# Four strided transfers in place of the first load of a one-token decode kernel

## The chip, the core and the metric

The kernel runs on one core of a Trainium2 chip. The engines of the core are TensorE (PE), VectorE (DVE), ScalarE (ACT), GpSimd (POOL) and SyncE (SP); sixteen DMA engines move data between HBM and the on-chip memory SBUF, which has 128 partitions. An instruction on one engine that needs the work of another waits on a semaphore. A transfer adds 16 to its semaphore when all of it has landed. The metric is the device time of one execution in microseconds (us), the median of several.

## What is computed

One token passes through a pre-norm transformer block whose attention reads a long cache of keys and values. All data are float32.

```python
def _A_ref(x, k_cache, v_cache, wq, wo):          # H = 32 heads, Sk = 8192, Dh = 192, D = 640
    q = (x @ wq).reshape(B, Sq, H, Dh).transpose(0, 2, 1, 3)
    scores = jnp.einsum("bhqd,bhkd->bhqk", q, k_cache) * (Dh ** -0.5)
    p = _softmax(scores, axis=-1)
    o = jnp.einsum("bhqk,bhkd->bhqd", p, v_cache)
    return o.transpose(0, 2, 1, 3).reshape(B, Sq, H * Dh) @ wo

h = x + _A_ref(_layernorm(x), A_k_cache, A_v_cache, A_wq, A_wo)
h2 = h + _B_ref(_layernorm(h), B_W_gate, B_W_up, B_W_down)   # gated ReLU, F = 1536
```

Keys and values of 32 heads are 2 x 32 x 8192 x 192 x 4 bytes, about 403 MB; with the weights the kernel reads 446 MB and writes 640 numbers.

## The kernel before

**Layout.** The host packs all inputs into arrays of 128 rows, so that every load takes one contiguous row for each partition. One large buffer, `big`, holds three places for loads (`place[0]` to `place[2]`, line 95), with eight columns ahead of them for x. A head's keys are 12,288 columns, 24 blocks of `QB` = 512 columns that TensorE multiplies with a masked query; its values are 12,288 columns too, which VectorE multiplies with the softmax weights and sums.

**The first array.** `first` holds, for each partition, eight columns with five numbers of x, then `WO` = 960 columns in which the query weights of head 0 lie, then the 12,288 columns of K for head 0, then the query weights of three more heads. It goes to the beginning of `big` in two loads. The first takes `FIRST` columns: x, the query weights and the first four blocks of K (semaphore `w0`). The second takes the rest (semaphore `r1`). Both destinations are the same columns of `big` as the source columns of `first`, so that `FIRST` only sets where the cut lies.

**Order of the loads.** All large loads are issued by SP, one behind the other, in `sync_fn` (the helper `load`, line 156). The start issues `w0`, `r1` and `r2` (values of head 0 and keys of head 1) with no wait between them. After these, `turn` (line 158) issues the loads of three heads for each pass of the loop, eleven passes in all (`NT`); each load waits until the compute engines are done with the place that it overwrites: V's load `r3` waits for `wo`, K's `r4` for `vk`, and so on. The weights of the second half (`ww`) come at the end in six pieces.

**What waits for the first load.** VectorE waits for `w0` (line 263) before it sums x; behind that lie the first layer norm, the five matmuls of head 0's query on TensorE (into `pq`), the columns of the query (`columns`, VectorE) and the masked queries `qs` on ScalarE (`masks`, lines 400 and 401). TensorE then waits for `r1` and for `qs` before the scores of head 0 (`scores`, which go through the helper at line 433). VectorE waits for `r1` before it multiplies the next heads' query weights (`weigh`, line 296). TensorE and VectorE wait for `r1` even for the blocks of K that `w0` has brought.

**Other queues.** ScalarE issues one small load of x for the residual (`xrow`) and one half of the output's store; SP issues the other half (line 188) and waits for both (line 194). GpSimd writes constants at the start and issues no transfer.

Of the kernel before, what the change touches and what calls it, by code (L numbers as in the profile page):

```python
# [10 lines left out]
P, Q, NQ = 128, 32, 4  # L11
# [6 lines left out]
QB = 512  # L18
# [6 lines left out]
WO = D + HN  # L25
# [13 lines left out]
RA, RB = VF + VF, KW + 2 * WO  # L39
R1 = WO + KW + 3 * WQ  # L40
LW = VL + 2 * WO
X0 = 8
FIRST = X0 + WO + 4 * QB

FW = 2 * DJ * F + FJ * D
GATE, DOWN = DJ * F, 2 * DJ * F
# [1 line left out]
CUTS = (0, GATE, DOWN, DOWN + 6 * D, DOWN + 10 * D, FW - HD, FW)  # L48
HOME = (X0 + 2 * RA, X0, X0 + RA + LW)
SCALE = DH ** -0.5  # L50
# [28 lines left out]
def mha_decode_reglu_kernel(nc, x, first, k0, k1, v1, k2, v2, v3, ww, out):  # L79
# [4 lines left out]
    s = {n: nc.alloc_semaphore("e_" + n) for n in names}  # L84
# [3 lines left out]
    def sb(name, shape):  # L88
        return nc.alloc_sbuf_tensor(name, shape, F32).ap()
# [3 lines left out]

    big = sb("big", [P, X0 + 2 * RA + RB])
    place = [big[:, X0:X0 + RA], big[:, X0 + RA:X0 + 2 * RA], big[:, X0 + 2 * RA:]]
    xrow = sb("xrow", [NQ, DG])
# [49 lines left out]
    def home(c0, n):  # L146
        m = min(c0 // GATE, 2)
        return big[:, HOME[m] + c0 - m * GATE:HOME[m] + c0 - m * GATE + n]
# [5 lines left out]
    def sync_fn(sy):  # L154
        def load(n, dst, src):
            sy.dma_start(dst, src).then_inc(s[n], 16)  # L156

        def turn(t, r1):
            sy.wait_ge(s["wo"], t)
            load("r3", place[0], v1[t - 1])  # L160
            sy.wait_ge(s["vk"], 2 * t)
            load("r4", place[1], k2[t - 1])
            load("r5", place[2], v2[t - 1])
            sy.wait_ge(s["op"], 3 * t)
            load("r1", place[0][:, 0:r1], k0[t - 1][:, 0:r1])
            sy.wait_ge(s["sp"], 3 * t)
            load("r2", place[1], k1[t])

        load("w0", big[:, 0:FIRST], first[:, 0:FIRST])
        load("r1", big[:, FIRST:X0 + R1], first[:, FIRST:])  # L170
        load("r2", place[1], k1[0])
        with sy.Fori(1, NT - 1) as t:
            turn(t, R1)
        turn(NT - 1, WO + KW + WQ)
        sy.wait_ge(s["wo"], NT)
        load("r3", place[0][:, 0:VF], v1[NT - 1][:, 0:VF])
        load("r3b", place[0][:, VF:], v1[NT - 1][:, VF:])
        sy.wait_ge(s["vk"], 2 * NT)
        load("r4", place[1][:, 0:LW], v3)
        for i, (c0, c1) in enumerate(zip(CUTS, CUTS[1:])):  # L180
            if c0 == GATE:
                sy.wait_ge(s["op"], H)
            load(f"ffn{i}", home(c0, c1 - c0), ww[:, c0:c1])
# [64 lines left out]
    def vector_fn(v):  # L248
# [11 lines left out]
        v.sem_inc(s["op"], 1)  # L260

        s1, mean, s2, var, rstd = (st[:, i:i + 1] for i in range(4, 9))
        v.wait_ge(s["w0"], 16)
        v.reduce_sum(s1, xT, axis=AX.X).then_inc(s["st"])
        v.wait_ge(s["st"], 2)
        stat(v.tensor_scalar_mul(mean, pt[:, 0:1], 1.0 / D))
# [252 lines left out]
    def tensor_end(t):  # L519
# [27 lines left out]
        ins.then_inc(s["pd"])  # L547

    sync_fn(nc.sync)
    scalar_fn(nc.scalar)  # L550
    pool_fn(nc.gpsimd)
    vector_fn(nc.vector)
    tensor_fn(nc.tensor)
    tensor_end(nc.tensor)
# [6 lines left out]
def _pack(x, k, v, wq, wo, up, gate, down):  # L561
# [23 lines left out]
    rows = [_np.zeros(z, k.dtype) for z in ((NT - 1, P, R1), (NT, P, RA), (NT, P, RA), (NT - 1, P, RA), (NT - 1, P, RB))]  # L585
    first = _np.zeros((P, X0 + R1), k.dtype)
    first[:, 0:DJ] = x.reshape(P, DJ)
# [43 lines left out]
```

## Time and profile before

| quantity | value |
|---|---|
| median of three runs | 1037.24 us (1037.07 to 1037.32) |
| device time of the profiled execution | 1037.36 us |
| its span in the profile | 1036.0 us |
| mean granted TensorE clock | 0.641 of full speed |
| read from HBM | 445.91 MB, 430 GB/s over the span |
| large loads: K, V, weights of the second half | 31, 23 and 6, beside the two of `first` |

A row of the page's groups gives the line, the engine, the operation and what it writes and reads. In the windows, each row gives a stretch's start and end, its length, the busy time of PE, weight load, DVE, ACT and POOL (with the count of instructions), the granted TensorE clock, the mean busy share of the DMA engines and the GB/s that they moved. In short windows the DMA columns scatter, since a packet's bytes are booked over its recorded time and some records overlap. In the timeline, the first two columns are start and duration; in brackets stands how long the engine had been idle and what released it. The list of DMA issues gives the size and the median time from issue to landing. The chain of waits is followed back from the last instruction, and its rows are start, length and what it was spent on.

### The profile page before, as it was taken

The page shows a single profiled execution, that of the slowest core. Times are in us where ns is not written, and L with a number is a line of the kernel's source. Part 1 is how long each engine was busy: PE and PEld are TensorE (multiplying, and loading weights), DVE is VectorE, ACT ScalarE, POOL GpSimd, SP SyncE. Part 2 cuts the span into 40 slices and gives each one's busy share as a digit, 9 for nine tenths or more (in the row PEclk, how much of TensorE's full clock was granted, in tenths as well). Part 3 has the DMA queues.
Part 4 walks back from the last instruction along what each step waited for, and adds up shares of the span by engine and source line. Part 5 has one row for each costly group of instructions (what it writes and reads, how often), then busy time and mean ns, then how long its engine had stood idle before and what let it go on. Part 6 is the DMA issues. An engine that isn't in the chain of part 4 may idle for free.

```text
span 1036.0 us, 6215 instructions
## 1 busy us (share of the span) xinstructions
PE 337.1 (33%) x2104; PEld 104.0 (10%) x2104; DVE 604.5 (58%) x1288; ACT 61.0 (6%) x145; POOL 3.5 (0%) x18
## 2 busy tenths in 40 slices
PE   3413323143323134240523322233315133231527
PEld 2100100010001001010100000010101001010103
DVE  3555737645675656476555747645666557376582
ACT  1000000000000000000000000000000000000010
POOL 1000000000000000000000000000000000000000
PEclk9756665666657566655666575666657566656667
DMA  9999999999999999999999999999999999999998
GB/s 400 444 443 418 430 443 424 456 410 443 440 441 410 438 445 441 410 449 431 443 410 439 441 443 430 417 444 443 411 437 443 443 415 432 443 424 439 428 433 348
DMA packets 8948, 445.98 MB, mean 430 GB/s; under 512 B 1000, under 2 KB 1136, under 8 KB 1264
## 3 DMA queue, kind: packets, MB, share of 16 engines
q1 hardware_dynamic: 8932, 445.92, 99.6%
q8 instruction: 3, 0.05, 0.0%
q14 instruction: 1, 0.01, 0.0%
q10 hardware_dynamic: 12, 0.00, 0.0%
HBM read 445.91 MB, written 0.00 MB: 430 GB/s over the span
## 4 chain that ended last, share of the span: by engine, by line
DMA 81%; DVE 10%; PE 8%; issue 0%; SPq 0%; ACT 0%
DMA big<-in_k_dram 76%; DVE big L151 9%; PE sp L433 8%; DMA big<-in_ww_dram 3%; DMA big<-in_v_dram 2%; PE pq L433 0%; DVE mp L315 0%; SPq L156 0%; DVE op L151 0%; PE acc L433 0%; PE pt L473 0%; ACT o L429 0%
## 5 line engine op out<-in xcount | busy, mean ns | idle before, releaser
L151 DVE CUSTOM_DVE_ANT_0 big<-big,p 128x1024 f32<-128x1024 f32 x384 | 445.0, 1221 | 276.3 <-DMA big<-in_v_dram 173.1
L433 PE MATMUL sp<-big,qs 128*32 128x512 f32 x1536 | 266.1, 858 | 398.7 <-DMA big<-in_k_dram 253.3
L433 PEld LDWEIGHTS sp<-big,qs 128*32 128x32 f32 x1536 | 60.0, 147 | 573.8 <-issue 256.8
L433 PE MATMUL po<-op,same 128*128 128x13 f32 x66 | 17.6, 343 | 237.8 <-DVE op L151 237.8
L405 ACT ACTIVATE p<-sp,m 128x1024 f32<-128x1024 f32 x32 | 35.7, 1114 | 928.7 <-DVE m L319 928.7
L315 DVE TENSOR_REDUCE mp<-sp 128x1 f32<-128x1024 f32 x32 | 39.2, 1225 | 55.9 <-PE sp L433 55.9
L433 PEld LDWEIGHTS po<-op,same 128*128 128x128 f32 x66 | 14.6, 274 | 251.2 <-DVE op L151 242.8
L288 DVE SCALAR_TENSOR_TENSOR big<-big,xn 128x576 f32<-128x576 f32 x44 | 35.8, 813 | 0.4
L296 DVE TENSOR_SCALAR big<-big,xn 128x576 f32<-128x576 f32 x11 | 6.8, 618 | 44.0 <-DMA big<-in_k_dram 37.2
L151 DVE DVE_READ_ACCUMULATOR2_ANT op<- 128x1 f32 x384 | 31.8, 83 | 0.0
L473 PE MATMUL pt<-ident,mp 128*128 128x128 f32 x32 | 11.1, 346 | 40.2 <-DVE mp L315 40.2
L291 DVE SCALAR_TENSOR_TENSOR big<-big,o 128x640 f32<-128x640 f32 x22 | 19.3, 878 | 0.0
L151 DVE CUSTOM_DVE_ANT_0 junk<-ident,pq 128x128 f32<-128x128 f32 x34 | 9.7, 285 | 11.1 <-PE pq L433 11.1
L243 DVE RECIPROCAL rl<-po 128x1 f32<-128x1 f32 x33 | 5.4, 165 | 13.0 <-PE po L433 13.0
L151 DVE CUSTOM_DVE_ANT_0 junk<-blk,po,rl 128x8 f32<-128x8 f32 x66 | 11.9, 218 | 1.2
L433 PE MATMUL pq<-big,ones 128*128 128x384 f32 (+1 forms) x44 | 12.5, 406 | 0.0
L292 DVE SCALAR_TENSOR_TENSOR big<-big,o 128x320 f32<-128x320 f32 x22 | 12.0, 545 | 0.0
L319 DVE TENSOR_REDUCE m<-pt 128x1 f32<-128x128 f32 x32 | 9.3, 290 | 4.6 <-PE pt L473 4.6
L400 ACT ACTIVATE qs<-pick,q 128x64 f32<-128x64 f32 x34 | 11.5, 338 | 3.8 <-DVE q L151 3.8
L473 PEld LDWEIGHTS pt<-ident,mp 128*128 128x128 f32 x32 | 4.5, 140 | 68.6 <-DVE mp L315 68.6
L401 ACT ACTIVATE qs<-pick,q 128x32 f32<-128x32 f32 x34 | 10.4, 306 | 0.0
L433 PE MATMUL sp<-big,hc 128*32 128x384 f32 x80 | 9.3, 616 | 0.6 <-DVE hc L371 0.6
(88 smaller groups left out, 106.7 us busy)
## 6 DMA issues: line engine op xcount, KB each, us to landing
big<-in_k_dram SPq DMA_DIRECT2D x9, 8064.0 KB, 31.0
big<-in_v_dram SPq DMA_DIRECT2D x10, 7104.0 KB, 45.7
big<-in_v_dram SPq DMA_DIRECT2D x2, 4096.0 KB, 22.7
big<-in_ww_dram SPq DMA_DIRECT2D x2, 3840.0 KB, 27.1
big<-in_k_dram SPq DMA_DIRECT2D x1, 7104.0 KB, 28.9
big<-in_first_dram SPq DMA_DIRECT2D x1, 6560.0 KB, 20.9
big<-in_v_dram SPq DMA_DIRECT2D x1, 3008.0 KB, 17.3
big<-in_ww_dram SPq DMA_DIRECT2D x1, 1920.0 KB, 32.4
```

The costliest lines, as they stand in the source:

```text
L151: return eng.tensor_tensor_reduce(out=res, in0=a, in1=b, scale=scale, scalar=0.0, op0=ALU.mult, op1=ALU.add, accum_out=dst)
L288: return v.scalar_tensor_tensor(tq, wqs[:, :, j, :], xn[:, j:j + 1], tq, op0=ALU.mult, op1=ALU.add)
L291: v.scalar_tensor_tensor(tw[:, 0:D], wos[i][:, 0:D], o[:, i, 0:1], tw[:, 0:D], op0=ALU.mult, op1=ALU.add)
L292: return v.scalar_tensor_tensor(tw[:, D:WO], wos[i][:, D:WO], o[:, i, 1:2], tw[:, D:WO], op0=ALU.mult, op1=ALU.add)
L296: v.tensor_scalar_mul(tq, tq, xn[:, 0:1]).then_inc(s["pr"])
L315: v.reduce_max(mp, sp, axis=AX.X).then_inc(s["mp"])
L319: v.reduce_max(m1, pt[:, 0:P], axis=AX.X, negate=True).then_inc(s["m1"])
L400: a.mul(qs[:, i, 0:2, :], pk[:, 0:2, :], q[:, i, 0:1])
L401: a.mul(qs[:, i, 2, :], pk[:, 2, :], q[:, i, 1:2]).then_inc(s["qs"])
L405: a.activation(p, sp, AF.Exp, bias=m1, accum_out=op[:, i, NJ:NJ + 1]).then_inc(s["rs"])
L433: return nc.tensor.matmul(dst, lhsT, rhs, start=start, stop=stop, **kw)
L473: t.transpose(pt[:, 0:P], mp.to_broadcast([P, P]), ident).then_inc(s["pt"])
```

## The change

`FIRST` grows from four to eight blocks of K, so that the cut between the two loads of `first` moves from column 3016 to column 5064. The load of the part ahead of the cut becomes four loads on the same queue and the same semaphore. Each takes a set of partitions at a regular step: partitions 0, 8, 16, ... (16 of them), then 4, 12, 20, ... (16), then 2, 6, 10, ... (32), then 1, 3, 5, ... (64). Together they are all 128. VectorE's wait for `w0` asks for 64 instead of 16. The loads behind them, their order and their waits stay.

```diff
 R1 = WO + KW + 3 * WQ
 LW = VL + 2 * WO
+LANES = ((0, 8), (4, 8), (2, 4), (1, 2))
 X0 = 8
-FIRST = X0 + WO + 4 * QB
+FIRST = X0 + WO + 8 * QB
...
-        load("w0", big[:, 0:FIRST], first[:, 0:FIRST])
+        for p0, step in LANES:
+            load("w0", big[p0:P:step, 0:FIRST], first[p0:P:step, 0:FIRST])
         load("r1", big[:, FIRST:X0 + R1], first[:, FIRST:])
         load("r2", place[1], k1[0])
...
-        v.wait_ge(s["w0"], 16)
+        v.wait_ge(s["w0"], 16 * len(LANES))
```

## The prediction

> **What bounds the kernel now.** I read the page first (engines' shares, queues), then the windows at the start and in the middle, the list of DMA issues, the start of the chain of waits and the timeline of the first 35 us, and last the end of the chain.
>
> ```profile
> span 1036.0 us, 6215 instructions
> PE 337.1 (33%) x2104; PEld 104.0 (10%) x2104; DVE 604.5 (58%) x1288; ACT 61.0 (6%) x145; POOL 3.5 (0%) x18
> ...
> q1 hardware_dynamic: 8932, 445.92, 99.6%
> ...
> DMA 81%; DVE 10%; PE 8%; issue 0%; SPq 0%; ACT 0%
> ```
> ```profile
> 0.00:2.00 2.00, 0.00 (x0) 0.00 (x0) 0.00 (x0) 0.58 (x1) 1.40 (x10) 1.00 0.20 37
> 2.00:4.00 2.00, 0.00 (x0) 0.00 (x0) 0.00 (x0) 0.70 (x1) 1.86 (x9) 1.00 0.85 308
> ...
> 100.00:900.00 800.00, 249.33 (x1487) 71.64 (x1487) 476.82 (x996) 42.51 (x104) 0.00 (x0) 0.63 1.00 433
> ```
>
> The queue that SP feeds is busy for 99.6% of the span on sixteen engines; no compute engine is above 58%. In the 800 us from 100 to 900 the DMA share is 1.00 at 433 GB/s, which is 433 / 16 = 27.1 GB/s for each DMA engine. So the chain's DVE and PE pieces lie beside a stream that never stops, and the kernel is as long as the stream: 445.92 MB at 433 GB/s are 1029.8 us. What remains of 1036.0 lies at the two ends. For that I need when the transfers were issued and landed.
>
> ```profile
> big<-in_first_dram SPq DMA_DIRECT2D x1, 6560.0 KB, 20.9
> ...
> big<-in_first_dram SPq DMA_DIRECT2D x1, 1508.0 KB, 5.9
> ```
> ```profile
> 0.81 0.42 SPq L156
> 1.23 0.06 issue
> 1.29 0.41 SPq L156
> 1.70 0.05 issue
> 1.75 40.50 DMA big<-in_k_dram
> ...
> 1032.35 0.04 issue
> 1032.39 1.93 PE pq L433 x56
> 1034.34 0.30 ACT o L429
> ```
>
> The first transfer (1508 KB) is issued at 0.81 and lands 5.9 us later, at 6.71. The second (6560 KB) is issued at 1.29 and lands at 22.19. Between the two landings 6.72 MB arrive in 15.48 us, 434 GB/s: the stream is at its steady rate right behind the first transfer. At that rate the first one's 1.544 MB take 3.56 us, so 5.9 - 3.56 = 2.34 us of its time is start: issue, first bytes, ramp and notice of landing. The tail, from the last large landing on the chain (1032.35) to 1036.0, is 3.65 us. Together 0.81 + 2.34 + 1029.8 + 3.65 = 1036.6, 0.6 over the span because the last weights still arrive within the tail. Whatever the change does to the start of the stream therefore moves the end by as much.
>
> **The change, part by part.** My sums are made against the profiled execution: span 1036.0, device time 1037.36 (1.36 beside the span). The median is 1037.24, 0.12 lower; I add the difference to the median.
>
> *Bytes.* The four transfers carry 20,256 B a partition, 2532 KB; the second falls from 6560 to 5536 KB. The sum is 8068 KB before and after: 0.
>
> *Issues.* SP issues three more. From the chain rows, one costs 0.42 + 0.06 us, so the second transfer goes out at 1.29 + 3 x 0.47 = 2.70 and K's next block at 3.16 instead of 1.75. The cover is the data of the four: 5.97 us at 434 GB/s. A 16-row transfer has, if it is spread over all sixteen engines, one row of 20,256 B for each, 0.75 us at 27.1 GB/s; that is longer than the 0.47 to the next issue, so no engine runs dry between them: 0. Without that cover the three would cost 1.41.
>
> *Completions.* Three more sets of sixteen. The 433 GB/s of the long window already contains those of its transfers; its rounding (0.5 in 433, 1.2 us over the kernel's 62 loads) leaves at most 0.02 each, or 0.06 us; I take that.
>
> *The later x.* VectorE's wait is now for 64 increments, all four transfers. Behind it in VectorE's queue are the layer norm and the first query, and TensorE and ScalarE wait for those. x comes 1024 KB later, 2.42 us.
>
> ```profile
> 6.75 0.16 DVE L264 TENSOR_REDUCE st<-big 128x1 f32<-128x5 f32 x1 [0.84 <-DMA big<-in_first_dram]
> ...
> 15.19 0.31 ACT L401 ACTIVATE qs<-pick,q 128x32 f32<-128x32 f32 x1
> ...
> 22.23 0.62 DVE L296 TENSOR_SCALAR big<-big,xn 128x576 f32<-128x576 f32 x1 [6.84 <-DMA big<-in_first_dram]
> ...
> 22.25 7.40 PE L433 MATMUL sp<-big,qs 128*32 128x512 f32 x48 [7.59 <-DMA big<-in_first_dram]
> ...
> 33.22 0.34 SPq L156 DMA_DIRECT2D big<-in_v_dram  x1
> ```
>
> The chain from x to the masked query ends at 15.50, and both engines then wait for the second transfer until 22.23. The slack is 6.7 us; 2.42 fit into it: 0. If the four transfers are slow, the second one lands late by the same amount, so the slack never falls under 6.7 - 2.4 = 4.3. Nor does the stream run dry later: V's first load is issued at 33.22 while K's block lands at 1.75 + 40.50 = 42.25, 9.0 us ahead, and both shift together.
>
> *The ramp* is what can be won. A small transfer that has almost no data shows the part of the 2.34 us that a transfer pays at any rate:
>
> ```profile
> 1034.67 0.34 SPq L188 DMA_DIRECT2D out_dram<-o  x1
> ```
> ```profile
> SPq L194 <- DMA out_dram<-o: 0.9, 1, 0.9
> ```
>
> The 1.2 KB store takes 0.34 + 0.9 = 1.24 us from issue to landing. So the ramp is at most 2.34 - 1.24 = 1.10 us, and a gain has that as its end; the other end is 0. The window from 2 to 4 us runs at 308 instead of 433: 125 x 2 us = 250 KB, 0.58 us. With one row an engine in the first transfer the engines may start closer together, but a first row must still be fetched from cold. I take -0.4, most of the 0.58 and not the 1.10.
>
> *The rate of part transfers* is the cost that decides, and the trace of before has no row for it: every load that fills the stream has 128 rows, and 433 GB/s is known for those alone. From below: the engines run at 27.1 GB/s whichever partitions they write, cost 0. From above: a transfer with every eighth partition reaches only half of SBUF's receiving side. If the 433 GB/s are sixteen receiving shares of 27.1, of which sixteen engines in a whole transfer take one each, then two engines meet at one share, the other shares stand idle, and the rate is 217. The engines work their queue in order, so the first two transfers (16 rows, 0.324 MB each) cost 0.75 more each, 1.49 together. In the 32-row and the 64-row transfer each engine has two and four rows. If an engine's rows follow each other in the transfer, all engines write first one half of the shares and then the other, and these double too: 1.49 and 2.99 more. All four: 5.97 us. An upper end that needs no such picture is a whole start for each added transfer, 3 x 2.34 = 7.0 (rival c); the two agree in size. Engines that are out of step relieve this: one that is 0.2 us ahead leaves the shared half 0.2 us earlier, at each of the six stretches (one, one, two, and two double ones), 1.2 us in all; the 0.2 is an estimate, a third of the ramp's 0.58. I take 5.97 - 1.2 = 4.8, near the upper end: a rate of exactly sixteen equal parts looks like a fixed share for each engine, and nothing in the diff keeps two engines off one share.
>
> [...]
>
> **The sum:** 0 + 0 + 0.06 + 0 - 0.4 + 4.8 = +4.5 us. Span 1040.5; on the median 1037.24 + 4.5 = **1041.7 us**.
>
> **The rivals.** About 0.2% (2.07 us) is what a measurement of this kernel can tell from no change; it lies at 1035.17 and 1039.31.
>
> (a) *Ramp alone, not slower.* Place: the first 4 us. Each engine gets its first row early, and any 16 engines run at 27.1 GB/s. For it speaks the window at 308 GB/s; against it that the stream then needs a rate which the trace shows for 128 rows only. Price -0.4 (0 to -1.1): 1036.8 (1036.1 to 1037.2). It decides if the part transfers keep over 95% of 433 GB/s (5% of 5.97 us is 0.3). That the split does nothing at all, since the engines take rows in the same way as before, ends here too.
>
> (b) *Only the two 16-row transfers are at half rate*, since with 32 and 64 rows the engines already spread over all shares at any moment: +1.49 + 0.06 - 0.4 = +1.1: 1038.4. [...] Against: it needs an order of rows in the engines that suits the stride.
>
> (c) *Each transfer pays a start of its own*, not hidden under the one ahead: 3 x 1.24 - 0.4 = +3.3: 1040.6. Against it: the second transfer follows the first at 434 GB/s, so its start was hidden under 3.6 us of data; the 16-row ones have only 0.75 us ahead of them. At most 3 x 2.34 = +7.0.
>
> (d) *Over 2.07 us won.* Needs more than the whole ramp of 1.10; only a change of the tail could add to it.
>
> **How the numbers follow.** Forecast 0.46, (a) 0.20, (b) 0.24, (c) 0.06, (d) 0.04. The forecast's own range runs from six tenths of the doubling (5.97 x 0.6 - 0.4 = +3.2, 1040.4) to all of it without relief and no ramp gain (+6.0, 1043.2). The whole range reaches down into (a), to 1036.5, leaving out (d) and the better half of (a), and up to 1043.0. Slower: the forecast less 0.02 for its mild end, and (c): 0.50. Within 0.2%: (a), (b) and that rest: 0.46. Faster: (d), 0.04.
>
> **What would show it.** Issue rows: four of `first` at 0.81, 1.28, 1.75, 2.2 and the 5536 KB one at about 2.7. The last of the four should land near 0.81 + 2.34 - 0.4 + 5.97 + 4.8 = 13.5 us (VectorE's first reduce on x at L264's place); by (a) at 8.7, by (b) at 10.2, by (c) at 12.1. The 5536 KB transfer, then, lands 5.669 MB / 434 = 13.1 us after it, 26.6 instead of 22.2, and every later landing is late by the same 4.5. The windows from 4 to 12 us should show some 220 to 260 GB/s. Wrong would be: windows back at 433 by 4 us; a first reduce before 9 us; a later landing that moves by another amount than the second transfer's; or VectorE and TensorE waiting for the masked query instead of for the second transfer at L296 and L433.

## The result, and the profile after

The changed kernel takes 1038.88 us (median of 22 runs, 1038.46 to 1039.63), the kernel before 1037.22 in the same sessions (22 runs, 1036.97 to 1037.48). The ratio is 1.0016, 95% interval 1.001 to 1.0023: 1.66 us slower, within 0.2%. The forecast was +4.5, so its direction holds and its size doesn't; rival (b) with +1.1 comes nearest.

The page of the changed kernel (span; busy time by engine; the load queue's packets, MB and share; the chain by engine):

```profile
span 1037.6 us, 6218 instructions
PE 334.1 (32%) x2104; PEld 103.5 (10%) x2104; DVE 604.3 (58%) x1288; ACT 61.0 (6%) x145; POOL 3.5 (0%) x18
...
q1 hardware_dynamic: 8980, 445.92, 99.5%
...
DMA 81%; DVE 10%; PE 8%; SPq 0%; issue 0%; ACT 0%
```

Nothing has changed in what bounds it: the same 445.92 MB, in 48 packets more (three completions on sixteen engines), the same 58% of VectorE. The windows of the start and of the middle, read as before (the last column is GB/s):

```profile
2.00:4.00 2.00, 0.00 (x0) 0.00 (x0) 0.00 (x0) 0.69 (x1) 1.86 (x9) 1.00 1.24 304
4.00:6.00 2.00, 0.00 (x0) 0.00 (x0) 1.53 (x8) 0.00 (x0) 0.26 (x1) 1.00 0.72 192
...
6.00:9.00 3.00, 0.00 (x0) 0.00 (x0) 0.00 (x0) 0.00 (x0) 0.00 (x0) 1.00 1.00 425
...
100.00:900.00 800.00, 247.16 (x1487) 71.32 (x1487) 478.12 (x998) 42.50 (x104) 0.00 (x0) 0.63 1.00 434
```

The steady stream runs at 434 GB/s, as it did at 433. The stretch from 4 to 6 us, in which the second 16-row transfer and the first rows behind it are moved, shows 192; from 6 to 9, where the 32-row and the 64-row transfer are under way, it is 425 already. The loss is made in about the first 6 us and then stays. (Such short windows scatter; the lengths of single packets, further down, say the same without that.) The list of DMA issues and the timeline say the same by landings:

```profile
big<-in_first_dram SPq DMA_DIRECT2D x1, 5536.0 KB, 20.5
...
big<-in_first_dram SPq DMA_DIRECT2D x1, 1266.0 KB, 8.1
big<-in_first_dram SPq DMA_DIRECT2D x2, 316.5 KB, 4.6
big<-in_first_dram SPq DMA_DIRECT2D x1, 633.0 KB, 5.7
```
```profile
10.82 0.16 DVE L266 TENSOR_REDUCE st<-big 128x1 f32<-128x5 f32 x1 [4.91 <-DMA big<-in_first_dram]
...
19.25 0.31 ACT L403 ACTIVATE qs<-pick,q 128x32 f32<-128x32 f32 x1
...
23.91 0.62 DVE L298 TENSOR_SCALAR big<-big,xn 128x576 f32<-128x576 f32 x1 [4.46 <-DMA big<-in_first_dram]
...
23.93 1.94 PE L435 MATMUL sp<-big,qs 128*32 128x512 f32 x8 [5.21 <-DMA big<-in_first_dram]
...
34.74 0.35 SPq L157 DMA_DIRECT2D big<-in_v_dram  x1
```

VectorE's first use of the second transfer (L298 here, L296 before) moves from 22.23 to 23.91, by 1.68. V's first load goes out at 34.74 instead of 33.22, by 1.52, and the span ends 1.6 later. One delay at the start is passed through the whole kernel. The masked query ends at 19.56, and both engines wait for the second transfer for 4.4 us more, so that the later x costs nothing.

### The profile page after: what moved, and what is told of

It reads as the page before. It is cut to its first block, busy times and chain, and to the rows that moved or that the text cites. A ratio compares the mean times of both kernels' runs of the same rounds, so it can differ in the third digit from the quotient of the medians.

```text
span 1037.6 us, 6218 instructions
## 1 busy us (share of the span) xinstructions
PE 334.1 (32%) x2104; PEld 103.5 (10%) x2104; DVE 604.3 (58%) x1288; ACT 61.0 (6%) x145; POOL 3.5 (0%) x18
## 3 DMA queue, kind: packets, MB, share of 16 engines
q1 hardware_dynamic: 8980, 445.92, 99.5%
## 4 chain that ended last, share of the span: by engine, by line
DMA 81%; DVE 10%; PE 8%; SPq 0%; issue 0%; ACT 0%
DMA big<-in_k_dram 76%; DVE big L152 9%; PE sp L435 8%; DMA big<-in_ww_dram 3%; DMA big<-in_v_dram 2%; SPq L157 0%; PE pq L435 0%; DVE mp L317 0%; DVE op L152 0%; PE acc L435 0%; PE pt L475 0%; ACT o L431 0%
## 5 line engine op out<-in xcount | busy, mean ns | idle before, releaser
L435 PE MATMUL sp<-big,qs 128*32 128x512 f32 x1536 | 263.2, 849 | 398.3 <-DMA big<-in_k_dram 254.6
L298 DVE TENSOR_SCALAR big<-big,xn 128x576 f32<-128x576 f32 x11 | 6.8, 618 | 41.7 <-DMA big<-in_k_dram 37.2
```

Source lines behind the costliest of these rows:

```text
L298: v.tensor_scalar_mul(tq, tq, xn[:, 0:1]).then_inc(s["pr"])
L435: return nc.tensor.matmul(dst, lhsT, rhs, start=start, stop=stop, **kw)
```

## The experiments

Each time stands beside that of the kernel before on the same chip in the same session.

**One transfer, the larger piece.** `LANES` holds one set with all partitions.

```diff
-LANES = ((0, 8), (4, 8), (2, 4), (1, 2))
+LANES = ((0, 1),)
```

> The first transfer is one again, of all 128 partitions, but with the changed kernel's 20 KB a partition (eight of K's blocks). Theory P (part transfers with every eighth partition run at half rate): no such transfer is left, so 1037.2, within 0.2 of the kernel before. Theory S (the larger first piece, and x that lands later with it, costs the time): as the changed kernel, 1038.9.

Measured: 1037.24 beside 1037.18, +0.06. The larger piece and the later x cost nothing; theory S falls.

**Four sets at a step of four.**

```diff
+LANES = ((0, 4), (1, 4), (2, 4), (3, 4))
```

> Four transfers of 32 partitions each, at steps of four from 0, 1, 2 and 3, of 20 KB a partition. Theory P (the slow rate is that of sets of partitions at a step of eight, which reach half of the receiving shares): a step of four reaches all, every packet takes 0.75 us, 1037.2 to 1037.5. Theory C (each of several transfers issued one after another at the cold start runs slow, whichever its partitions): 1038.9 or more, first packets at 1.4 us as in the changed kernel. Theory I (three more issues and the longer issue of a strided transfer cost the time): +1.7, the same as the changed kernel.

Measured: 1037.76 (1037.55 to 1038.10) beside 1037.18 (1037.05 to 1037.39): +0.58. The two ranges don't meet, though the interval of the ratio (0.9996 to 1.0014) still holds 1. It is above theory P's 1037.5 by a little, and a third of the changed kernel's loss with the same number of transfers. C and I, which ask for +1.7, fall as causes of the whole; what is left of them is the 0.58. The windows of this kernel, at the place of the 192:

```profile
4.00:6.00 2.00, 0.00 (x0) 0.00 (x0) 1.53 (x8) 0.00 (x0) 0.26 (x1) 1.00 1.00 405
```

**Eight sets at a step of eight.**

```diff
+LANES = ((0, 8), (4, 8), (1, 8), (5, 8), (2, 8), (6, 8), (3, 8), (7, 8))
```

> Eight transfers of 16 partitions each, all at a step of eight, of 20 KB a partition. Theory P: all eight rows of each engine at half rate, 8 x 0.75 = +6.0 us, less the ramp: 1042.7 to 1043.4. Theory C: only what is moved in the first 4 us is slow, so +1.7: 1038.9. Theory I: four more issues than the changed kernel, each 0.6 us, hidden under data: 1039 to 1040.

Measured: 1042.43 beside 1037.18, +5.25. The loss grows with the rows that are moved in such sets and not with the time since the start; C falls for good. P's range began 0.3 higher. One window across these transfers shows the rate:

```profile
4.00:12.00 8.00, 0.00 (x0) 0.00 (x0) 1.53 (x8) 0.00 (x0) 0.26 (x1) 1.00 1.02 236
```

**Two halves of neighbouring partitions.**

```diff
-LANES = ((0, 8), (4, 8), (2, 4), (1, 2))
+LANES = ((0, 64), (64, 128))
...
-        for p0, step in LANES:
-            load("w0", big[p0:P:step, 0:FIRST], first[p0:P:step, 0:FIRST])
+        for p0, p1 in LANES:
+            load("w0", big[p0:p1, 0:FIRST], first[p0:p1, 0:FIRST])
```

> Two transfers of neighbouring partitions, 0 to 63 and 64 to 127, of 20 KB a partition. Theory P, if the shares are groups that repeat within 64 partitions: each reaches half of the shares and the whole 2.59 MB goes at half rate, +6.0 us: 1042.7 to 1043.4. If it is the step of eight itself that is slow (descriptors or HBM rows eight apart): 1037.2. Theory C: one more transfer at the start, 1037.2 to 1037.8.

Measured: 1043.66 beside 1037.18, +6.48. No step is in it, and it is slower than the eight sets at a step of eight. So the cost isn't one of the step itself; it goes with the partitions that a transfer covers.

```profile
6.00:9.00 3.00, 0.00 (x0) 0.00 (x0) 0.00 (x0) 0.00 (x0) 0.00 (x0) 1.00 1.00 216
```

216 is half of 433, as it would be with half of the receiving shares idle. The column ahead of it, the mean busy share of the sixteen DMA engines, stands at 1.00: all sixteen are at work, at 216 / 16 = 13.5 GB/s each where 433 / 16 is 27.1, so it isn't that half of the engines go unused.

**The changed kernel's four sets in a warm stream.** This run starts from the kernel before (four blocks of K in the first transfer). The first transfer is whole, the second (52,480 B a partition) is split. Three of its parts have a semaphore of their own, `x1`; VectorE and TensorE wait for that just ahead of their loops.

```diff
-        load("r1", big[:, FIRST:X0 + R1], first[:, FIRST:])
+        for i, (p0, step) in enumerate(LANES):
+            load("x1" if i + 1 < len(LANES) else "r1", big[p0:P:step, FIRST:X0 + R1], first[p0:P:step, FIRST:])
```

> The first transfer as before (one, 12 KB a partition); the second one, 52,480 B a partition, is split into the changed kernel's four sets (step eight from 0, step eight from 4, step four from 2, step two from 1). It runs behind other data, in a warm stream. Theory P: the two sets at a step of eight cost one row of 1.94 us each more, the others nothing: +3.9, 1041.1. Theory C (the loss belongs to the cold start of the stream): within 0.3 of the kernel before, 1037.2 to 1037.5.

Measured: 1041.53 beside 1037.23, +4.30, against P's +3.9. With the stream running the two 16-row sets are just as slow, and at a larger row they cost more. By the trace's records of single packets (one packet is one partition's row) a row of the two sets takes 3.58 and 3.86 us, where one of the same size takes 1.94 in the next run. The first rows behind them take 2.37 before they are back at 1.94. These are 1.64 + 1.92 + 0.43 = 4.0 us, which is what the profiled execution lost (1041.24 us); P's sum has no third term. The window across the two sets:

```profile
7.00:14.00 7.00, 4.73 (x15) 4.26 (x16) 2.11 (x12) 1.78 (x3) 0.00 (x0) 1.00 0.86 225
```

**The same split with a step of four.** `LANES = ((0, 4), (1, 4), (2, 4), (3, 4))` in the kernel of the run before this one.

> As the run with the second transfer in the changed kernel's four sets, but with four sets at a step of four (from 0, 1, 2 and 3). Theory P: no set at a step of eight, all shares reached, 1037.2 to 1037.5. If any split of a warm transfer costs (issues, completions, rows further apart in HBM): +3.9 as there, or a part of it.

Measured: 1037.27 beside 1037.23. In a warm stream four transfers instead of one cost nothing that can be seen (+0.04), if each is a set at a step of four. The same window as above:

```profile
7.00:14.00 7.00, 5.09 (x16) 4.55 (x16) 1.95 (x11) 1.78 (x3) 0.00 (x0) 1.00 0.99 427
```

225 and 427 GB/s at the same place of the stream, with the same bytes and the same number of transfers, are the plainest pair of the study. In this run the packets of all eight rows of an engine take 1.94 us.

**Neighbouring rows of HBM.** The host stores the rows of `first` in the order of the sets (columns up to `FIRST` alone), and the sources become plain ranges.

```diff
+        r0 = 0
         for p0, step in LANES:
-            load("w0", big[p0:P:step, 0:FIRST], first[p0:P:step, 0:FIRST])
+            rz = r0 + len(range(p0, P, step))
+            load("w0", big[p0:P:step, 0:FIRST], first[r0:rz, 0:FIRST])
+            r0 = rz
...
+    order = [p for p0, step in LANES for p in range(p0, P, step)]
+    first[:, 0:FIRST] = first[order, 0:FIRST]
```

> The changed kernel's four transfers to the same partitions, but the host stores their rows one behind the other, so that each transfer reads neighbouring rows of HBM. Theory P (the half rate is on the receiving side): as the changed kernel, 1038.7 to 1039.1, packets of the two 16-row sets 1.38 us. Theory H (HBM rows that lie eight apart, 516 KB, are what is slow): no half rate is left, 1037.8 as with four sets at a step of four, packets 0.75 us.

Measured: 1038.90 beside 1037.19, +1.71, as the changed kernel's +1.66. H falls: with the source in order the loss is the same, and of the two theories P is left, which puts it on the side that receives.

**Four blocks instead of eight.** `FIRST = X0 + WO + 4 * QB` in the changed kernel.

> The changed kernel's four sets with the kernel before's 12 KB a partition (four blocks of K). Theory P, with relief of about 0.2 us at each of two stretches: the two slow rows cost 2 x (0.45 - 0.2) = 0.5 in place of 2 x (0.75 - 0.2) = 1.1, beside the 0.6 that four sets at a step of four cost: 1038.3. A fixed cost of each transfer: 1038.9 as the changed kernel. Engines that run dry between the issues (0.62 apart, rows of 0.45): above 1038.9.

Measured: 1038.11 beside 1037.19, +0.92; P expected 1038.3, and a fixed cost or dry engines 1038.9 and more. The loss falls with the size of the rows.

**Two sets at a step of two, and four whole transfers by columns.** The first has `LANES = ((0, 2), (1, 2))`; the second is:

```diff
-        for p0, step in LANES:
-            load("w0", big[p0:P:step, 0:FIRST], first[p0:P:step, 0:FIRST])
+        for c0 in range(0, FIRST, FIRST // 4):
+            load("w0", big[:, c0:c0 + FIRST // 4], first[:, c0:c0 + FIRST // 4])
```

> Two transfers of 64 partitions, even and odd ones, 20 KB a partition. Theory P: both reach all shares, no slow row after the start. Theory N (the rest of the loss, 0.6 us with four sets at a step of four, is the slower issue and later start of a transfer that has fewer than 128 partitions, once, at the start): 1037.6 to 1037.8. If it is a cost of each added transfer, a third of 0.6: 1037.4.

> Four transfers again, but each of all 128 partitions and a quarter of the columns (5 KB a partition). Theory N: issue 0.42 us and first packets as in the kernel before, 1037.2. If three more transfers at the start cost 0.6 whatever their partitions: 1037.8. If short first rows make the ramp shorter: 1036.6 to 1037.0.

Measured: 1037.59 and 1037.54 beside 1037.19, +0.40 and +0.35. Sets of 64 rows at a step of two are not at half rate, and short first rows win nothing. These differences are about as large as the ratios can tell (both 1.0003, 0.9994 to 1.0012), but the traces show them as landings: VectorE's first use of the second transfer is at 22.73 and 22.57, after 22.29 with one whole transfer of the same size. These are the rows, the one transfer's first, then the step of two, then the columns:

```profile
22.29 0.62 DVE L298 TENSOR_SCALAR big<-big,xn 128x576 f32<-128x576 f32 x1 [4.46 <-DMA big<-in_first_dram]
```
```profile
22.73 0.62 DVE L298 TENSOR_SCALAR big<-big,xn 128x576 f32<-128x576 f32 x1 [4.46 <-DMA big<-in_first_dram]
```
```profile
22.57 0.62 DVE L298 TENSOR_SCALAR big<-big,xn 128x576 f32<-128x576 f32 x1 [4.47 <-DMA big<-in_first_dram]
```

The packet records put the two losses in different places. The first packet starts at 1.84 or 1.85 us wherever the first transfer has all 128 partitions (the kernel before, one larger transfer, four by columns), and at 2.13 to 2.22 in every kernel whose first transfer has fewer. At a step of two the sixteen first rows end 0.34 us later than with one transfer (mean 3.65 and 3.31), and the rows of the second transfer start 0.36 later (8.94 and 8.58): the loss is there at once, as theory N has it. The four transfers by columns start in time, but a row of 5 KB takes 0.195 us, where a quarter of a 20 KB row would be 0.188. Over the 32 short rows of each engine that is 0.2 us. So theory N's late start is borne out; its 1037.2 for the columns is not, since the short rows lose that 0.2 beside it.

**Eight sets at a step of eight, the sides taken one after the other.**

```diff
+LANES = ((0, 8), (1, 8), (2, 8), (3, 8), (4, 8), (5, 8), (6, 8), (7, 8))
```

> The eight sets at a step of eight again, in another order: starting partitions 0, 1, 2, 3, 4, 5, 6, 7 instead of 0, 4, 1, 5, 2, 6, 3, 7. Theory P with shares by groups of four neighbouring partitions: sets 0 to 3 press on one half of the shares and 4 to 7 on the other, so that engines out of step relieve each other once instead of seven times; as the two halves, 1043.2 to 1043.7. If the relief is no matter of the sides changing: as the eight sets before, 1042.4. If the groups are not of four neighbours (each single partition has a share of its own): 1042.4 too, or another time altogether.

Measured: 1043.68 beside 1037.28, +6.40. The same eight transfers in another order lose 1.2 us more, as much as the two halves (+6.48). That is what theory P expects if partitions 0 to 3 of each eight press on one half of the shares and 4 to 7 on the other: the loss is 5.25 where the sides change seven times and 6.40 where they change once.

**Row by row.** The packet records show this most directly. All these kernels move 128 rows of 20,256 B ahead of the second transfer, eight for each DMA engine. The packets are put in order of start and taken sixteen at a time, one for each engine; the table has the median length of each sixteen in us, and the start of the first packet.

| kernel | first start | 1st | 2nd | 3rd | 4th | 5th | 6th | 7th | 8th |
|---|---|---|---|---|---|---|---|---|---|
| one transfer | 1.84 | 1.21 | 0.75 | 0.75 | 0.75 | 0.75 | 0.75 | 0.75 | 0.75 |
| four sets at a step of four | 2.14 | 1.46 | 0.77 | 0.75 | 0.75 | 0.75 | 0.75 | 0.75 | 0.75 |
| two sets at a step of two | 2.15 | 1.33 | 0.76 | 0.75 | 0.75 | 0.75 | 0.75 | 0.75 | 0.75 |
| the changed kernel | 2.22 | 1.35 | 1.38 | 1.20 | 0.75 | 0.75 | 0.76 | 0.75 | 0.75 |
| eight sets, sides alternating | 2.19 | 1.22 | 1.37 | 1.38 | 1.39 | 1.38 | 1.38 | 1.39 | 1.39 |
| eight sets, one side first | 2.19 | 1.30 | 1.55 | 1.57 | 1.57 | 1.39 | 1.57 | 1.57 | 1.58 |
| two halves | 2.13 | 1.37 | 1.48 | 1.60 | 1.59 | 1.38 | 1.58 | 1.60 | 1.58 |

A row at full rate takes 0.75 us, in one transfer as at a step of four or two. Behind the first rows, a row of a set at a step of eight or of a contiguous half takes 1.48 to 1.60, and 1.37 to 1.39 where the set before it lay on the other side: in the second row of the changed kernel, in every row of the alternating sets, and in the fifth of the last two kernels. That engines out of step cause this relief fits, but nothing here shows it by itself. The first rows take 1.2 to 1.5 us in every kernel, whichever partitions they cover.

No run beat the kernel before; the single larger piece and the warm split at a step of four only equal it.

## Why the prediction failed, point by point

**Bytes, the later x, the shift of everything behind: right.** The one larger transfer is level with the kernel before (+0.06). The slack of the masked query was put at 4.3 us or more and is 23.91 - 19.56 = 4.35. A delay of the second transfer (+1.68) comes out at the end (+1.6 in the span, +1.66 in the median).

**The 16-row transfers: right in the half rate and in the sum, with some luck.** Two rows at half rate were put at 1.49 us, with 0.2 of relief at each of two stretches 1.1. The changed kernel less the four sets at a step of four is 1.66 - 0.58 = 1.08. The picture behind it, receiving shares of which such a transfer reaches half, had no row of before behind it; the runs show what it asks for: 216 GB/s in the halves, 225 beside 427 in the warm pair, and the same loss with the HBM rows in order (+1.71 beside +1.66), so on the receiving side. The terms lie elsewhere than in the working, though. The first slow row costs nothing that can be seen beside a start that is slow with any partitions (1.35 us, 1.46 at a step of four); the second costs 0.6 (1.38 for 0.77), and the first row of the 32-row set, which starts while other engines are still at the second set, 0.4 (1.20 for 0.75). The relief is real: eight sets lose 5.25 where the sides alternate and 6.40 where they don't, and the rows differ by 1.57 - 1.38 = 0.2. That the estimate was 0.2 is luck, since a third of the ramp's 0.58 has nothing to do with it.

**The 32-row and 64-row transfers: wrong, and this is the step that failed.** The prediction took 1.49 + 2.99 us more for them, less the relief of their four stretches, on the assumption that an engine's rows follow each other in the transfer, so that all engines would write one half of the shares and then the other. They cost nothing of the kind: the window from 6 to 9 us stands at 425 GB/s, the rows of the changed kernel take 0.75 us from the fourth on, sets at a step of four alone cost 0.04 us in a warm stream, and sets at a step of four or two 0.40 to 0.58 at the start. In the picture of shares, the rows of such sets are then dealt to the engines so that all shares are at work at any moment. Two simple orders don't fit that: neighbouring rows to one engine, which the prediction took, and one row to each engine in turn, since the first sixteen rows would then lie in partitions 0 to 63, the half that ran at 216 GB/s. How the assignment is made, the trace doesn't say. Rival (b) had this right and was given 0.24.

**Issues and ramp: wrong in sign, by 1 us.** I took 0 for the issues, at 0.47 us from one to the next, and -0.4 for the ramp. Several transfers in place of the first cost +0.35 to +0.58 instead, and the window from 2 to 4 us still shows 304 GB/s (308 before). A part is visible in the chain's first rows of the changed kernel:

```profile
0.81 0.62 SPq L157
1.43 0.06 issue
1.49 0.57 SPq L157
2.06 0.05 issue
2.11 0.58 SPq L157
```

The first issue takes 0.62 us instead of 0.42, and nothing runs beside that one which could hide it; the issues lie 0.62 to 0.68 us apart. The first packet starts at 2.22 instead of 1.84, so the longer issue is 0.20 of a delay of 0.38. Four sets at a step of four show the same, 2.14 instead of 1.84: their sixteen first rows end 0.39 us later than with one transfer (mean 3.70 and 3.31), which is two thirds of their 0.58. The other 0.19 comes in among their later rows, and its cause stays open. Four whole transfers start in time and lose their 0.35 otherwise, mostly in rows that are a quarter as long.

**Put together:** of the +1.66, +0.58 is what four part transfers at the start cost without a set at a step of eight, and the +1.08 beside it belongs to the two at a step of eight. Against the sum of +4.5, the 32-row and the 64-row transfer were 3.7 too high (1.49 + 2.99 less 0.8 of relief) and the ramp 1.0 too low. Rival (b) missed 0.5 by the ramp, which it took as a gain, less the relief that it left out. The first reduce on x came at 10.82, near (b)'s 10.2 and far from the forecast's 13.5. Rival (c)'s own terms give a landing at 12.4, not the 12.1 of the prediction; nothing hangs on it.

## What to carry to other kernels

Before a load is cut by partitions, ask which partitions each piece covers, since the number of rows didn't decide here: 32 at a step of four or 64 at a step of two kept the full rate (0.75 to 0.77 us for a row behind the first), while 16 at a step of eight or 64 neighbouring ones ran at about half (1.37 to 1.60 us). Cutting by columns left all 128 partitions in each piece, but its rows of 5 KB ran about 4% slower for their size (0.195 us for 0.188). In the middle of a full queue a cut at a step of four was free (+0.04 us); at the start of the stream every cut that was tried cost 0.35 us or more. In this kernel, which is one unbroken stream of loads, a delay in the first microseconds was paid in full at the end (+1.68 us at the second transfer's landing, +1.66 in the time), and nothing downstream won it back.

## What was not expected of the hardware

A first transfer of fewer than 128 partitions took longer to issue in these runs, however it was cut: 0.56 us for 64 neighbouring partitions, for 32 at a step of four and for 64 at a step of two, 0.60 to 0.62 for 16 at a step of eight, against 0.42 for all 128. Later issues don't show this cleanly, since a whole transfer behind part transfers took 0.59 too. The first packet of such a transfer started at 2.13 to 2.22 us, against 1.84 or 1.85 with all 128.

The half rate was not a fixed price for a set: the same eight 16-row transfers took 5.25 or 6.40 us more, by the order in which they were issued.
